# The second block's layer held behind the attention's scores, and its rows' transposes in the layer's own PSUM tiles

## The chip, the cores and the metric

The kernel runs on one NeuronCore of a Trainium2 chip. The metric is the device time of one execution in microseconds (us), lower is better. TensorE is called PE, VectorE DVE, ScalarE ACT, GpSimd POOL and SyncE SP, as in the profile.

## What is computed

Three stages follow each other: an attention over 4 batches of 12 heads (448 tokens, 64 dimensions a head) with a root-mean-square norm on q and k, a gated layer on the 1792 tokens, and a mixture of 8 experts that sends each token to the one with the largest logit.

```python
q_n, k_n = (rmsnorm(q, g_q), rmsnorm(k, g_k))
scores = (1.0 / np.sqrt(64)) * np.matmul(q_n, k_n.transpose(0, 1, 3, 2))
attn = softmax(scores)                       # the row's maximum is subtracted
x = heads_side_by_side(np.matmul(attn, v))   # 1792 x 768
gate = 1.0 / (1.0 + np.exp(-(x @ w_gate)))
x = (gate * (x @ w_val)) @ w_out             # d_ff = 1536
idx = np.argmax(cosine(x, expert_emb) / tau, axis=1)
for e in range(8):
    h = np.maximum(x[idx == e] @ w1[e], 0.0)
    out[idx == e] = gate_w[idx == e, None] * (h @ w2[e])
```

## The kernel before

All products are in float32 precision: a matrix is split into a high and a low part, and three products of parts are summed, so a layer tile is 18 matmuls of 448 columns (six input blocks, three products).

**The attention** (`attention`, L451) works on head pairs g = 0 to 23; six of them are one batch, called a block here. A head pair has eight steps u (four groups of 112 tokens, two heads). The generator yields three times a step. For head pair g the steps are: `maxima` (L364), a first score product whose row maxima DVE takes (tiles m{g}_{u}); at step 7 `shifts` (L372), which transposes the negated maxima on PE (pm{g}) and copies them on ACT into the shift rows X2 (L379, two copies); ten steps later than the maxima, `scores` (L386), two matmuls a step: the score itself (the first half, L392) and the shift with the low part (the second half, L393), after which ACT takes the exponential (L395) into pt{g}_{r}. `weigh` (L413) multiplies four exponentials at a time with v on PE (av{g}, "a weighing" below), and ACT copies the finished one (L429); `over_sums` divides by the sums (rb{g}). For the head pairs that follow, `q_side` and `k_side` transpose the normed q and k (pq, pk), and ACT and DVE copy them into X (L315) and Y (L358, L322); ACT also takes the squares of q and k (L263) and a small sum (ms, L271).

PSUM has eight tiles of one bank each, by tag: "mm" two, "T" three, "S" two, "av" one. The scores alternate between the two tiles of "S": score r takes the tile of score r - 2, which its exponential must have read. The maxima of head pairs 6 and up, pq, pk, pm and rb share the three of "T".

**The layer** of a block (`glu`, L689) runs beside the attention of later blocks: block 0 beside head pairs 6 to 11, block 1 beside 12 to 23. For each of 12 blocks of d_ff it makes two tiles of 18 products (pg{b}_{f}, pv{b}_{f}) in the tag "mm", the gate on ACT and DVE, and then six output tiles (po{b}_{d}) of 36 products each. `rows_of` (L987) turns each output tile, in two halves (px{b}_{d}_{h}), into rows of tokens, with the router's logits beside them; ACT copies the rows (L1004), and SP stores them. The products of all of them are issued by line L684 to L685.

**The third and fourth block** have one layer together (`glu_pair`, L784). Its first seven products for a weight block f are pa11, pa12, pa22, ps2, ps4, ps3 and ps1, nine matmuls each, of weights in four forms a, b, c, d; c and d are sums of weights that DVE forms and ACT casts (wh73c is the second weight block's c). pa11 and pa12 need only the third block's outputs (xhp, xlp); the others need sums of outputs of both blocks (tht, tlt, thb, tlb), the last of them those of head pair 23.

**The order of the work.** A scheduler with a simulated timeline puts the instructions in order for each engine; within an engine they then run in that order. The driver at the end of `tile_kernel` only sets the order in which the work is offered: 288 steps of the attention's generator for block 1, and the layer's 37 steps spread over them:

```python
while done * (ticks + (SLACK1 if b else SLACK)) < (i + 1) * n_side:
    next(side, None)
    done += 1
```

What is offered earlier has precedence, but an instruction whose inputs are not ready is passed by, so the layer's products fill PE wherever the attention waits. `tc.issue_after(x)` makes what is issued inside it, on x's engine, stand behind x in that engine's order; it adds no wait on the chip.

Of the kernel before, what the change touches and what calls it, by code (L numbers as in the profile page):

```python
# [20 lines left out]
B, H, S, D = 4, 12, 448, 64  # L21
CP = 112
NCH = S // CP
NG = 2 * NCH
# [40 lines left out]
SPL = ("AD","AD","AD")  # L65
SLACK = 2
SLACK1 = 50
START = 155
RAT = (4, 5, 13, 17, 26)
R3 = (28, 44)  # L70
# [36 lines left out]
def tile_kernel(ctx, tc, q, k, v, g_q, g_k, w_gate, w_val, w_out, emb, tau, w1, w2, out):  # L107
    nc = tc.nc
# [9 lines left out]
    def psum(tag, bufs, name):  # L118
        return ps.tile([P, 512], F32, tag=tag, name=name, bufs=bufs)
# [10 lines left out]
    last = {}  # L130
# [90 lines left out]
    def stage(g):  # L221
        return 0 if g < H // 2 else 1 if g < H else 2
# [163 lines left out]
    def scores(g, r, st):  # L386

        kc, j = divmod(r, 2)
        s_ = psum("S", 2, f"s{g}_{r}")
        z = slice(kc * CP, (kc + 1) * CP)  # L390
        yh, yl = st["Y"][j]
        nc.tensor.matmul(s_[:CP, :S], lhsT=yh[:, z], rhs=st["X"][j], start=True, stop=False)  # L392
        nc.tensor.matmul(s_[:CP, :S], lhsT=yl[:, z], rhs=st["X2"][j], start=False, stop=True)  # L393
        p_ = a2.tile([CP, S], F32, tag="PT", name=f"pt{g}_{r}", bufs=NPT)
        last["exp"] = nc.scalar.activation(p_, s_[:CP, :S], AF.Exp)  # L395
        st["PT"][j, kc] = p_
        if kc and ADDS[stage(g)][r - 2] == "E":
            st["more"][j].append(p_)
        elif kc:
            eng = {"P": nc.gpsimd, "D": nc.vector}[ADDS[stage(g)][r - 2]]  # L400
            if kc == 1:
                st["sum"][j] = a2.tile([CP, S], F32, tag="sum", name=f"sum{g}_{j}", bufs=NSUM)
            eng.tensor_tensor(st["sum"][j], p_, st["PT"][j, 0] if kc == 1 else st["sum"][j], ALU.add)  # L403
# [47 lines left out]
    def attention():  # L451
# [9 lines left out]
        for t in range(NTICK):  # L461
# [16 lines left out]
            if 0 <= w < np_:  # L478
                scores(w, r, st[w])
# [182 lines left out]
    def step_feed():  # L662
        return next(feeders[-1], 1)

    def feed_to(n):
        while len(fed) < n and step_feed() is None:
            pass
# [21 lines left out]
    def glu(b):  # L689
# [31 lines left out]
        for d in range(NC_):  # L721
            pt = psum("mm", 2, f"po{b}_{d}")
            for h in range(2):
                n = NF // 2
                three(pt, n, S, piece(), gs[h * n:(h + 1) * n], h == 0, h == 1)
                if h == 0:
                    yield
            x2 = gp.tile([P, S], F32, tag="x2", name=f"x2{b}_{d}", bufs=2)
            nc.scalar.activation(x2, pt[:, :S], AF.Copy, scale=0.5)
            xT.append(x2)  # L730
            if d:
                rows_of(b, d - 1, xT[d - 1], ss6, lg)
            yield
        rows_of(b, NC_ - 1, xT[NC_ - 1], ss6, lg)
        side_jobs.append(route_all(b, ss6, lg))
        yield
# [47 lines left out]
    def glu_pair():  # L784
# [66 lines left out]
        for what, *at in pair_order():  # L851
# [23 lines left out]
            if h:  # L875
                ws[d] = w
                if d == 0:

                    steps = [second_steps(t, 0) for t in range(2)]
                    for k in (3 * (NF // 2 - 2), 99):  # L880
                        for m in steps:
                            for _ in zip(range(k), m):
                                pass
                    for t, x2 in enumerate(xT):
                        rows_of(b + t, d, x2, ss6[t], lg[t])
                    xT.clear()
                    yield
                elif d < NC_ - LATE:
                    for t in range(2):
                        rows_of(b + t, d, second_half(t, d), ss6[t], lg[t])  # L890
                        yield
                continue
# [94 lines left out]
    def rows_of(b, d, x2, ss6, lg, later=False):  # L987

        both = state["beside"][d % 2]
        nc.gpsimd.tensor_copy(both[:, P:], state["enT"][:, d])  # L990
        place = ROWS[d] if b == 1 else "r"
        rows = gp.tile([CP, NCH, P], F32, tag="rows", name=f"rows{b}_{d}", bufs=2) if place == "r" else \
            wp.tile([CP, NCH, P], F32, tag={"w": "wr", "s": "sq64"}[place], name=f"rows{b}_{d}", bufs={"w": 3, "s": SQB}[place])
        for h in range(2):
            tp = psum("T", 3, f"px{b}_{d}_{h}")
            z = slice(2 * h, 2 * h + 2)
            t_ = tp[:CP, :2 * (P + E)].rearrange("p (c d) -> p c d", c=2)
            for c in range(2):
                nc.tensor.matmul(t_[:, c], lhsT=x2[:, (2 * h + c) * CP:(2 * h + c + 1) * CP], rhs=both, start=True, stop=True)
            if d == 0:  # L1000
                nc.vector.tensor_copy(lg[:, z], t_[:, :, P:])
            else:
                nc.vector.tensor_tensor(lg[:, z], lg[:, z], t_[:, :, P:], ALU.add)
            nc.scalar.copy(rows[:, z], t_[:, :, :P])  # L1004
        nc.sync.dma_start(x2d[b * S:(b + 1) * S, d * P:(d + 1) * P].rearrange("(p c) d -> p c d", c=NCH), rows)

        def squares():
            rsq = gp.tile([CP, NCH, P], F32, tag="rsq", name=f"rsq{b}_{d}", bufs=1)
            if b:
                nc.scalar.activation(rsq, rows, AF.Square)  # L1010
            else:
                nc.gpsimd.tensor_tensor(rsq, rows, rows, ALU.mult)
            nc.vector.tensor_reduce(ss6[:, :, d:d + 1], rsq, axis=AX.X, op=ALU.add)

        if not later:
            squares()
        return squares
# [494 lines left out]
    def open_pool(name, **kw):  # L1512
        held = ExitStack()
        return held.enter_context(tc.tile_pool(name=name, bufs=2, **kw)), held
# [6 lines left out]
    for i in range(n_first):  # L1521
        next(att)
        if i == SETUP:
            with tc.issue_after(last["exp"].ins):
                router_setup()
        if i >= START and (i - START) % FSP == 0 and len(fed) < LEAD:
            with tc.issue_after(last["max"].ins), tc.issue_after(last["exp"].ins):
                step_feed()
    n_side = 2 * NF + 2 * NC_ + 1
    n_feed = 2 * NF + 2 * NC_  # L1530
    for b in range(2):
        side = glu(b)
        done = given = 0
        per = 6 if b == 0 else 2
        ticks = step * (b + 1)
        for i in range(ticks):
            next(att, None)
            if b == 0 and n_first + i == SETUP:
                with tc.issue_after(last["exp"].ins):
                    router_setup()  # L1540
            if n_first + b * step + i == 3 * (NG * H * B // 2 - 1) + CLOSE:
                a1_held.close()
            while given * ticks < (i + 1) * (n_feed * per + XF * b) and len(fed) < used[0] + LEAD + 1:
                step_feed()
                given += 1
            while done * (ticks + (SLACK1 if b else SLACK)) < (i + 1) * n_side:
                next(side, None)
                done += 1
        more = iter(())
        if b == 1:  # L1550
            for _ in att:
                pass
            a2_held.close()
            s1, s1_held = open_pool("s1", side="right", reuse_waits="tile")
            s2, s2_held = open_pool("s2", reuse_waits="tile")
            more = pair_inputs()
        for _ in side:
            feed_to(used[0] + LEAD)
            next(more, None)
        for _ in more:  # L1560
            pass
# [27 lines left out]
```

## Time and profile before

| what | value |
|---|---|
| time, median of 3 runs | 1205.92 us |
| lowest and highest of them | 1203.11 and 1209.46 us |
| the profiled execution's own time | 1203.91 us |
| its span, first to last instruction | 1202.2 us |
| PE, DVE, ACT, POOL busy | 95%, 70%, 56%, 43% |
| mean granted PE clock | 0.989 |

The span is what the trace shows of the execution; its own time is 1.7 us longer. In the trace a matmul of 448 columns has a duration of about 0.36 us, while the next one starts 0.2 us after it: the starts tell the rate, and idle time is counted only beyond the modelled ends. Stages: block 0's layer ends before 345 us, block 1's layer runs from there to about 625 us, and the pair's layer and the experts follow.

### The profile page before, as it was taken

The numbers are of one execution on the slowest core, as the hardware profiler recorded it, in microseconds if no ns is written. First come the engines' busy times: TensorE is split into PE (matmuls) and PEld (weight loads), VectorE is DVE, ScalarE is ACT, GpSimd is POOL, SyncE is SP. The second block draws the span as 40 slices with busy tenths as digits, with TensorE's granted clock in tenths as the row PEclk, the third lists the DMA queues.
The fourth block names the chain that finished last, engine by engine and source line by source line (L and its number), as shares of the span: only waits on it lengthen the run. The fifth ranks groups of instructions, "written<-read, shape, count | busy, mean of one in ns | idle before, by whom it ended". The sixth has DMA issues, their size and how long they took to land. (4 is left out here: it accounts for less than half of the span.)

```text
span 1202.2 us, 18401 instructions
## 1 busy us (share of the span) xinstructions
PE 1137.4 (95%) x6516; PEld 943.6 (78%) x6517; DVE 844.6 (70%) x1424; ACT 674.2 (56%) x1257; POOL 520.4 (43%) x425
## 2 busy tenths in 40 slices
PE   3998899899889999999998999999999999999996
PEld 2544677677667787776488999999998999999996
DVE  6888888878769866676888984197446566555652
ACT  5889776778665665665764333233323545555552
POOL 4897974679557646545731330043103111111001
PEclk9999899999999999999999999999999999999998
DMA  4212676666733222220131211111255675777763
GB/s 121 62 46 88 209 235 210 195 214 205 228 105 98 87 79 89 89 75 20 43 111 54 80 53 67 40 64 55 73 152 185 180 215 165 231 233 226 213 201 102
DMA packets 151106, 156.15 MB, mean 130 GB/s; under 512 B 6947, under 2 KB 135205, under 8 KB 151010
## 3 DMA queue, kind: packets, MB, share of 16 engines
q1 hardware_dynamic: 148034, 143.07, 39.2%
q0 software_dynamic: 2848, 11.74, 2.8%
q8 instruction: 53, 0.87, 0.3%
q14 instruction: 43, 0.35, 0.1%
q10 hardware_dynamic: 128, 0.11, 0.0%
HBM read 129.74 MB, written 25.91 MB: 129 GB/s over the span
## 5 line engine op out<-in xcount | busy, mean ns | idle before, releaser
L589 DVE TENSOR_TENSOR wl<-wr,wh 128x768 fp32r<-128x768 f32 (+1 forms) x194 | 187.6, 968 | 140.6 <-ACT wh L586 107.0
L586 ACT CAST wh<-wr 128x768 fp32r<-128x768 f32 (+1 forms) x212 | 171.6, 809 | 186.0 <-PE py L685 48.2
L370 DVE TENSOR_REDUCE nm<-m 112x1 fp32r<-112x448 f32 x192 | 114.1, 614 | 32.1 <-PE m L369 30.5
L395 ACT ACTIVATE pt<-s 112x448 f32<-112x448 f32 x192 | 101.2, 541 | 53.8 <-PE s L393 51.2
L403 POOL TENSOR_TENSOR sum<-pt,sum 112x448 f32<-112x448 f32 x78 | 104.1, 1342 | 37.5 <-ACT pt L395 36.9
L272 POOL TENSOR_TENSOR ms<-ms,mhalf 112x8 f32<-112x8 f32 x46 | 84.8, 1843 | 47.1 <-ACT ms L271 46.8
L418 PE MATMUL av<-pt,v 112*64 112x448 f32 x384 | 87.6, 567 | 1.6 <-ACT pt L395 1.6
L369 PE MATMUL m<-Y,X 128*112 128x448 f32 x192 | 72.7, 412 | 14.3 <-ACT X L315 4.9
L403 POOL TENSOR_TENSOR sum<-pt,pt 112x448 f32<-112x448 f32 x48 | 61.0, 1275 | 48.3 <-ACT pt L395 42.8
L392 PE MATMUL s<-X,Y 128*112 128x448 f32 x192 | 78.5, 409 | 2.2 <-ACT pt L395 2.1
L393 PE MATMUL s<-X,Y 128*112 128x448 f32 x192 | 71.7, 381 | 3.3 <-ACT X L379 3.3
L1297 POOL DMA_INDIRECT xe<-x2d,iu_all x16 | 19.0, 1190 | 123.9 <-PE pxe L1322 120.4
L392 PEld LDWEIGHTS s<-X,Y 128*112 128x112 f32 x192 | 34.3, 179 | 40.6 <-issue 31.7
L369 PEld LDWEIGHTS m<-Y,X 128*112 128x112 f32 x192 | 33.7, 182 | 37.9 <-ACT Y L322 8.0
L629 DVE SCALAR_TENSOR_TENSOR wr<-r,wr 128x768 int32<-128x768 int32 x36 | 57.8, 1607 | 0.6
L627 DVE SCALAR_TENSOR_TENSOR wr<-r 128x768 int32<-128x768 int32 x36 | 40.3, 1119 | 24.9 <-ACT r L624 22.3
L1308 POOL DMA_INDIRECT out_dram<-orow,iu_all x16 | 17.9, 1122 | 84.9 <-ACT orow L1429 76.6
L418 PEld LDWEIGHTS av<-pt,v 112*64 112x64 f32 x384 | 22.8, 138 | 36.1 <-issue 23.1
L685 PE MATMUL ph<-xeh,wh 128*128 128x256 f32 (+2 forms) x336 | 50.2, 284 | 0.0
L685 PE MATMUL ph<-xel,wh 128*128 128x256 f32 (+2 forms) x336 | 49.7, 282 | 0.0
L589 POOL TENSOR_TENSOR wl<-wr,wh 128x768 fp32r<-128x768 f32 x18 | 37.5, 2084 | 28.2 <-ACT wh L586 28.1
L685 PE MATMUL ph<-xeh,wl 128*128 128x256 f32 (+2 forms) x336 | 49.4, 282 | 0.0
(776 smaller groups left out, 3039.0 us busy)
## 6 DMA issues: line engine op xcount, KB each, us to landing
wr<-in_w_dram SPq DMA_DIRECT2D x112, 384.0 KB
wr<-w SPq DMA_DIRECT2D x72, 384.0 KB
w<-wr SPq DMA_DIRECT2D x36, 384.0 KB
r<-in_w_gate_dram SPq DMA_DIRECT2D x12, 768.0 KB
r<-in_w_val_dram SPq DMA_DIRECT2D x12, 768.0 KB
r<-in_w_out_dram SPq DMA_DIRECT2D x12, 768.0 KB
wr<-in_w_dram SPq DMA_DIRECT2D x24, 256.0 KB
v<-in_v_dram SPq DMA_DIRECT2D x24, 224.0 KB
```

The source lines that it names most:

```text
L272: nc.gpsimd.tensor_tensor(m, m, mhalf[:CP, :m.shape[1]], ALU.pow)
L369: nc.tensor.matmul(s_[:CP, :S], lhsT=st["X"][j][:, c * CP:(c + 1) * CP], rhs=st["Y"][j][0], start=True, stop=True)
L370: last["max"] = nc.vector.tensor_reduce(st["nm"][:, 2 * c + j:2 * c + j + 1], s_[:CP, :S], axis=AX.X, op=ALU.max, negate=True)
L392: nc.tensor.matmul(s_[:CP, :S], lhsT=yh[:, z], rhs=st["X"][j], start=True, stop=False)
L393: nc.tensor.matmul(s_[:CP, :S], lhsT=yl[:, z], rhs=st["X2"][j], start=False, stop=True)
L395: last["exp"] = nc.scalar.activation(p_, s_[:CP, :S], AF.Exp)
L403: eng.tensor_tensor(st["sum"][j], p_, st["PT"][j, 0] if kc == 1 else st["sum"][j], ALU.add)
L418: beside(*(lambda j=j, kc=kc: nc.tensor.matmul(st["av"][part_of(j), :S], lhsT=st["v"][:, j, kc], rhs=st["PT"][j, kc], start=0 in kcs and k ...
L586: nc.scalar.copy(hi, raw)
L589: eng.tensor_tensor(lo, raw, fv(hi), ALU.subtract)
L629: nc.vector.scalar_tensor_tensor(out=m, in0=high, scalar=-0x80000000, in1=m, op0=ALU.bitwise_and, op1=ALU.bitwise_or)
L685: nc.tensor.matmul(pt[:, :cols], lhsT=wts[i][a], rhs=xs[i][z], start=first and k == 1, stop=last and k == 3 * n)
```

## The change

It has two parts. The halves of `rows_of` for block 1 take their PSUM tile from the tag "mm" (two tiles, the ones in which the layer's products alternate) instead of "T" (three). And the driver keeps a list of marks, one for each step of the attention's generator: the last score matmul (second half) issued by then. In block 1 each step of the layer is issued behind the mark of 24 steps of the generator back, that is of eight scores back; it holds only instructions on the mark's engine, which is PE.

```diff
+AHEAD = 3 * NG
...
-        nc.tensor.matmul(s_[:CP, :S], lhsT=yl[:, z], rhs=st["X2"][j], start=False, stop=True)
+        last["s"] = nc.tensor.matmul(s_[:CP, :S], lhsT=yl[:, z], rhs=st["X2"][j], start=False, stop=True)
...
-            tp = psum("T", 3, f"px{b}_{d}_{h}")
+            tp = psum(*(("mm", 2) if b == 1 else ("T", 3)), f"px{b}_{d}_{h}")
...
+    marks = []
     for b in range(2):
...
             next(att, None)
+            marks.append(last["s"].ins)
...
-                next(side, None)
+                with tc.issue_after(marks[-AHEAD]) if b and len(marks) >= AHEAD else nullcontext():
+                    next(side, None)
                 done += 1
```

The number of instructions is the same; their order differs on every engine, on PE from tile pv1_4 of block 1's layer to the pair's first products. Lines of the change are one to seven higher than those of the kernel before.

PE before, from the transposes of k for head pair 19 to the first maximum of that pair (names: pk transposed k, s{pair}_{step} a score, pm the transposed maxima, pv and po tiles of the layer, av a weighing, m a maximum); rows that only repeat a tile are left out:

```order
L351 MATMUL pk19_4735<-ident_72,kn19_4573 128x112 x4
L392 MATMUL s17_7_4815<-X17_1_4171,Y35_4282 112x448
L393 MATMUL s17_7_4815<-X23_146,Y25_158 112x448
L376 MATMUL pm18_4748<-identr_134,nm0_136 66x112 x4
L685 MATMUL pv1_11_5521<-xh1_4_3510,wh59_5296 128x448
L392 MATMUL s18_0_4827<-X18_0_4403,Y36_4506 112x448
L685 MATMUL pv1_11_5521<-xh1_5_3514,wh59_5296 128x448
L685 MATMUL po1_0_5616<-gh1_0_3631,wh60_5380 128x448
L418 MATMUL av17_4730<-pt17_7_4818,v17_4389 64x448
L393 MATMUL s18_0_4827<-X20_140,Y20_148 112x448
L369 MATMUL m19_0_4761<-Y38_4740,X19_0_4650 112x448
```

Between pm18 and the second half of score 18_0 stood 14 products of pv1_11, nine of po1_0 and the weighing of pair 17. PE in the change, the same place:

```order
L419 MATMUL av17_4730<-pt17_4_4727,v17_4389 64x448
L370 MATMUL m18_7_4721<-Y37_4510,X18_1_4406 112x448
L393 MATMUL s18_1_4842<-X18_1_4406,Y37_4510 112x448
L352 MATMUL pk19_4735<-ident_72,kn19_4573 128x112 x4
L377 MATMUL pm18_4748<-identr_134,nm0_136 66x112 x4
L394 MATMUL s18_0_4827<-X20_140,Y20_148 112x448
L394 MATMUL s18_1_4842<-X21_142,Y21_150 112x448
L370 MATMUL m19_0_4761<-Y38_4740,X19_0_4650 112x448
L393 MATMUL s18_2_4896<-X18_0_4403,Y36_4506 112x448
L394 MATMUL s18_2_4896<-X20_140,Y20_148 112x448
L686 MATMUL pg1_9_5105<-xh1_0_3494,wh54_4890 128x448
```

The layer is at pg1_9 here, where it was at pv1_11 and po1_0; its 17 products follow score 18_2, and nothing of it stands between pm18 and that score. ACT in the change, the same place (xf the copy of a weighing, Y the copies of pk, kn the square of k, X20 and X21 the two copies of pm18, pt the exponential):

```order
L430 COPY xf17_4836<-av17_4730 128x448
L359 CAST Y38_4740<-pk19_4735 64x448
L264 ACTIVATE kn20_4794<-kr20_4585 112x2x4x64
L380 CAST X20_140<-pm18_4748 2x448
L380 CAST X21_142<-pm18_4748 2x448
L323 CAST Y38_4740<-Y38_4740 64x448
L359 CAST Y39_4744<-pk19_4735 64x448
L272 ACTIVATE ms20_4792<-ms20_4792 112x8
L396 ACTIVATE pt18_0_4830<-s18_0_4827 112x448
```

Before, the copies of pk19 and pm18 stood well ahead of the copy of the weighing; now they stand behind it. PE in the change at the start of the pair's layer, where rows that only repeat a tile are left out:

```order
L686 MATMUL po1_5_6204<-gh1_11_5543,wl71_6181 128x448
L1001 MATMUL px1_4_0_6286<-beside0_1247,x21_4_6161 112x136 x2
L686 MATMUL ps20_0_6412<-tht2_0_6129,wh72c_6235 128x448
L686 MATMUL pa220_0_6398<-tht4_0_6139,wh72b_6227 128x448
L686 MATMUL ps30_0_6441<-tht3_0_6134,wh72d_6239 128x448
L686 MATMUL pa221_0_6516<-tht4_0_6139,wh73b_6304 128x448
L686 MATMUL pa110_0_6372<-xhp0_6102,wh72a_6223 128x448
L686 MATMUL pa120_0_6383<-xhp3_6114,wh72a_6223 128x448
L686 MATMUL pa111_0_6490<-xhp0_6102,wh73a_6300 128x448
L686 MATMUL pa121_0_6501<-xhp3_6114,wh73a_6300 128x448
L686 MATMUL ps21_0_6530<-tht2_0_6129,wh73c_6312 128x448
```

Before, pa110 followed po1_5 directly and pa120 and pa111 came next, mixed with the sums' products; now all four tiles of pa11 and pa12 stand between pa221 and ps21.

## Rows read from the trace of the kernel before

**Rows 1.** The page's head: span, and each engine's busy time.
```profile
span 1202.2 us, 18401 instructions
PE 1137.4 (95%) x6516; PEld 943.6 (78%) x6517; DVE 844.6 (70%) x1424; ACT 674.2 (56%) x1257; POOL 520.4 (43%) x425
```

**Rows 2.** Windows: us; busy PE, PEld, DVE, ACT, POOL; PE clock; DMA share; GB/s.
```profile
540.00:550.00 10.00, 10.00 (x53) 8.79 (x53) 5.74 (x10) 4.07 (x9) 2.15 (x2) 1.00 0.08 24
570.00:580.00 10.00, 8.64 (x44) 4.61 (x44) 9.38 (x17) 8.77 (x19) 10.00 (x9) 1.00 0.08 23
640.00:650.00 10.00, 6.87 (x26) 5.87 (x25) 7.52 (x20) 2.85 (x5) 1.40 (x1) 0.83 0.16 40
```

**Rows 3.** Waits of PE, 556 to 602 us: total us, times, longest.
```profile
PE s L393 <- ACT X L379: 2.1, 2, 1.2
PE m L369 <- ACT Y L322: 1.5, 2, 1.2
PE av L418 <- ACT pt L395: 1.0, 2, 0.7
```

**Rows 4.** Timeline of PE, 572 to 576 us: start, us, instruction, idle before.
```profile
572.96 0.39 PE L376 MATMUL pm<-identr,nm 112*66 112x112 f32 x4
...
574.92 0.89 PE L393 MATMUL s<-X,Y 128*112 128x448 f32 x2 [1.20 <-ACT X L379]
```

**Rows 5.** Timeline of ACT, 571 to 575 us.
```profile
571.45 0.52 ACT L358 CAST Y<-pk 64x448 fp32r<-64x448 f32 x1
...
573.79 0.53 ACT L429 COPY xf<-av 128x448 f32<-128x448 f32 x1
574.35 0.95 ACT L379 CAST X<-pm 2x448 fp32r<-2x448 f32 x2
```

**Rows 6.** Timeline of PE, 530 to 540 us.
```profile
530.74 1.38 PE L685 MATMUL po<-gh,wl 128*128 128x448 f32 x6
531.96 0.37 PE L685 MATMUL po<-gh,wh 128*128 128x448 f32 x1
...
533.57 0.38 PE L376 MATMUL pm<-identr,nm 112*66 112x112 f32 x4
533.88 1.72 PE L418 MATMUL av<-pt,v 112*64 112x448 f32 x8
...
536.03 1.39 PE L685 MATMUL po<-gl,wh 128*128 128x448 f32 x6
537.26 1.40 PE L685 MATMUL po<-gh,wl 128*128 128x448 f32 x6
...
539.33 0.56 PE L393 MATMUL s<-X,Y 128*112 128x448 f32 x2
```

**Rows 7.** Timeline of all engines, 596 to 599 us.
```profile
596.34 1.72 PE L418 MATMUL av<-pt,v 112*64 112x448 f32 x8 [0.23 <-ACT pt L395]
...
598.11 0.54 ACT L429 COPY xf<-av 128x448 f32<-128x448 f32 x1 [1.82 <-PE av L418]
```

**Rows 8.** Timelines of PE and of ACT, 580 to 583 us.
```profile
580.78 0.37 PE L393 MATMUL s<-X,Y 128*112 128x448 f32 x1
...
581.25 0.55 ACT L395 ACTIVATE pt<-s 112x448 f32<-112x448 f32 x1 [0.31 <-PE s L393]
```

**Rows 9.** Timeline of PE, 645 to 651 us.
```profile
645.54 1.34 PE L685 MATMUL ps<-tht,wh73c 128*128 128x448 f32 x3 [3.13 <-ACT wh73c L586]
...
648.92 0.88 PE L685 MATMUL ps<-tht,wh72d 128*128 128x448 f32 x3
649.64 0.78 PE L685 MATMUL ps<-tlt,wh72d 128*128 128x448 f32 x3
650.25 0.78 PE L685 MATMUL ps<-tht,wl72d 128*128 128x448 f32 x3
```

**Rows 10.** Timelines of POOL at 650 and of ACT at 655 us.
```profile
650.67 1.02 POOL L1100 TENSOR_TENSOR ss<-ss,half 112x4 f32<-112x4 f32 x1 [7.41 <-DVE ss L1099]
...
655.88 0.23 ACT L1105 ACTIVATE ex<-lg 112x32 f32<-112x32 f32 x1
```

**Rows 11.** Waits of PE, 660 us to the end: the longest.
```profile
PE pxa L1241 <- DMA xea<-x2d,iua: 0.5, 1, 0.5
```

## The prediction

> **What bounds the kernel now.** I read the page first: TensorE (PE) is busy 95% of the 1202.2 us span [rows 1], so the time can move only through PE's idle time and clock. The windows show where the work that this change touches has any [rows 2]: at 540 to 550 us, where the second block's layer runs beside the attention, PE is full; at 570 to 580, where that layer has run far ahead and the attention's last head pairs are alone, it is busy 8.64 of 10 us; at 640 to 650, where the last two blocks' paired layer begins, 6.87 at a granted clock of 0.83. The list of waits names them: 2.1 us for the shift rows X (L379), 1.5 for Y (L322), 1.0 for the exponentials (L395), together 4.6 us between 556 and 602 us [rows 3].
>
> The timeline shows what such a wait is. At the border between two head pairs the shifts `pm` are transposed at 572.96, one maximum follows, and the next score's second half starts only at 574.92, after 1.20 us of idling for ACT [rows 4]. ACT was not waiting for `pm`: it was working through its own row of copies, one started every 0.58 us (571.45 to 574.35, five steps), and the copies of `pm` stand last [rows 5]. The same border earlier costs nothing: `pm` at 533.57, the score's second half at 539.33, and PE was full between, because the layer's products stood there, twelve of them in two of the rows, beside a weighing [rows 6]. A product is 0.203 us on PE (six in 530.74 to 531.96) [rows 6], a whole layer tile of 18 is 3.7 us. The cover is what hides the 2 to 3 us that ACT needs.
>
> **What the order shows.** The hold binds. In the changed order each tile of 18 products stands in one piece (at most one or two split off), directly behind the score that its mark names: pg1_9's mark is the score 18_2, and its first product follows that score's second half. Before, the products lay in the attention's gaps. Now, at the borders of head pairs 15, 17, 18, 19, 20 and 21, the tile that could cover has already run or is not yet allowed, and `pm` and the next scores stand next to each other; borders 16, 22 and 23 keep a weighing or products between. So the gaps of the stretch 556 to 602 are not filled; they are spread over some 190 us ahead of 600.
>
> **The terms.** *Removed:* the waits of the attention's lonely end, 4.6 us [rows 3].
>
> *Added at the borders.* Head pair 18 in full, t = 0 when PE leaves av17. ACT can copy av17 at about 0.1 (in the row, 0.05 us after the weighing's end) [rows 7]. `pk19` ends near 1.05, so Y38 starts at 1.1; behind it, at 0.58 a step [rows 5], the square of k for pair 20 at 1.7, the two copies of `pm18` from 2.3 (0.95 for both) to 3.2, then Y38's second half, Y39, ms20 (0.2) and, at about 4.5, the exponential of score 18_0, which takes 0.55 [rows 8]. Score 18_2 needs the bank that this exponential empties: it starts at 5.0. PE has in that time five matmuls at 0.2 and two groups of four transposes at 0.3 (533.57 to 533.88) [rows 6]: 1.7 us. So 3.3 us of waiting. The same count gives 1.0 at pair 15, 1.9 at 17, 1.6 at 19, 2.1 at 20 and 2.0 at 21: 11.9 us. Ends: six times the dearest single wait shown, 1.20 [rows 4], is 7.2; six times the 3.3 of pair 18 is 20. I keep the count, since it gives the shown 1.20 when applied to that border.
>
> *Added inside head pairs.* Scores 17_4, 22_4 and 23_2 stand behind one score or less since the score whose bank they take. The exponential ends 0.82 us after PE is free of a score (580.98 to 581.80) [rows 8], PE has 0.2 to 0.4 us of work: 0.4, 0.4 and 0.6. And the six casts of the paired layer's inputs stand on ACT between the exponentials 20_2 and 20_3; the weighing of pair 20 then waits about 1.0. Together 2.4; ends 0 and 5.
>
> *The paired layer's start.* There PE waited 3.13 us for the cast of a weight sum and then ran nine products in 3.38 us instead of 1.84 (three in 0.61) at the lower level of its clock [rows 9], 1.2 instead of 2.4 GHz: 4.7 us in all. In the changed order the 36 products (7.4 us) that need none of the summed inputs, pa110 to pa121, no longer come first but stand directly ahead of the one that waited, so they cover that cast; and pair 23's last weighing stands before all of the last layer tile (36 products) instead of before a third of it, so the inputs' chain on DVE begins 24 products, 4.9 us, earlier. A new wait appears: the fourth of these tiles, pa121, needs pa120's bank, which DVE empties only behind the routing's small instructions, with a POOL power of 1.02 us and an ACT exponential of 0.23 between them [rows 10]. I take 1.0 (ends 0 and the 4.7 removed, which would be a full exchange). Net -3.7.
>
> *The rows' transposes.* Each half now takes one of the two banks that the products alternate in, instead of one of three others. The next product tile waits for its copy on ACT. In the order 18 or more products or a weighing lie between such a half and the tile that takes its bank, over 3 us against one copy; nothing, upper end 0.5 per tile, 3 in all. The last two halves keep their banks until ACT has cast four more weights; pa110 starts behind that, level with PE's own arrival, and counts as nothing. The banks given up serve the maxima, whose waits are not in the list [rows 3]: no gain. The stores of the rows are issued earlier on SP and the layer's weight loads later, between the attention's own loads; POOL's subtractions for the layer move behind the attention's sums. None of them is waited for in the list, DMA is 0.08 busy at 540 to 550 and at 570 to 580 [rows 2], and what uses them moved back as far: nothing.
>
> *Sum:* -4.6 + 11.9 + 2.4 - 3.7 = **+6.0 us**. Behind 660 us PE's waits are some tenths each, the longest 0.5 us [rows 11], so whatever is won or lost reaches the end in full. The profiled execution took 1203.91 us, so 1209.9; the median of the three runs is 2.0 above it, 1205.92, and on that footing I say **1212.0 us**.
>
> **Rivals.** *Faster: the even mixture pays.* If ACT reaches each border with an empty queue and the scheduler's placement is right, the borders cost the 0.5 us that a copy of `pm` alone takes (half of 0.95): six times 0.5 is 3.0, the inner waits nothing, and -4.6 + 3.0 - 4.7 gives -6.3: 1199.6. For it: ACT is only 41% busy beside the layer at 540 to 550 [rows 2]. Against: the copies' order on ACT is fixed, and at each of the six borders the copy of the weighing and up to three others stand ahead of those of `pm`. It decides where all added waits stay under 3.3 us. The Trainium skill (Perfetto Trace Analysis, Optimization Strategy) says that a kernel with several regimes may gain by interleaving them, which is what is done here; by that rule the time comes out near this rival. The trace agrees only where the products lie between `pm` and the score [rows 6].
>
> *No measurable change.* The borders overlap more than counted (7.2, the lower end) and the inner waits halve: -4.6 + 7.2 + 1.2 - 3.7 = +0.1, so 1206.
>
> *Slower still: the clock.* After the 3.13 us wait the granted level fell and cost 1.54 us [rows 9]; the 1.20 us wait did not lower it (1.00 at 570 to 580) [rows 2]. Pair 18 idles 3.3 us in four parts with single matmuls between, pairs 17, 20 and 21 about 2. If the level falls at these four, 6.2 us come on top: 1218. It would need these waits to act as that one did. The Trainium skill (TensorE: Matmul & The Clock Gate, A second HAM failure mode) reports a kernel that lost clock to frequent short idling between its matmul groups; by it this rival would be the rule. The trace does not bear it out at 570 to 580, where the wait of 1.20 us lies.
>
> That the hold does nothing is excluded by the order.
>
> **How the numbers follow.** Half a per cent (6.0 us) is about what a measurement of this kernel can tell from no change. My forecast (+3 to +10) has 0.46, of which 0.29 lies beyond +6; no measurable change 0.25; the faster rival 0.15, counted whole as faster though its price lies only just beyond -6; the clock 0.14. So faster 0.15, same 0.17 + 0.25 = 0.42, slower 0.29 + 0.14 = 0.43. The range 1200 to 1220 leaves out the outer half of the two extreme cases, 0.08 and 0.07. The likeliest case alone gives 1209 to 1216.
>
> **What would show it.** Right: the waits of PE between 410 and 610 us sum to about 14 us, the largest for X (L380 then), Y and the exponentials, in groups every 25 us or so, each ahead of a solid tile of layer products; windows there fall from 10.00 to 9.2 or 9.5; the 3.13 us wait for wh73c is gone and the clock at the paired layer's start stays 1.00. Wrong: waits there under 8 us in sum (then faster or equal); a granted clock under 1.00 between 410 and 600 (then the clock rival); or a new wait of 3 us or more in the paired layer's first 30 us, which would take the gain there back.

## The result, and the profile after

The change makes the kernel slower by about 1%: 1216.93 us in the median of 6 runs (1215.76 to 1219.71), against 1206.58 us for six runs of the kernel before; the ratio is 1.0096, 95% interval 1.0079 to 1.0113. The profiled execution took 1215.76 us, its span is 1214.0 us: 11.8 us more than the span before. The head of its page answers to [rows 1]; each engine has as many instructions as before:

```profile
span 1214.0 us, 18398 instructions
...
PE 1140.6 (94%) x6516; PEld 945.4 (78%) x6517; DVE 842.2 (69%) x1424; ACT 676.9 (56%) x1257; POOL 525.6 (43%) x425
```

Two marks frame the changed part in both traces: the routing of the first block (`ppos`, at 405.88 us before and 405.69 now), up to which the order is the same, and the first product with wh78a, the eighth weight block of the paired layer (713.23 and 724.28 us). Between them lie 307.35 us before and 318.59 now, 11.24 more; 0.8 more comes behind, and ahead it is 0.2 less. These are the windows of the kernel after in which PE idles or its clock is under 1.00 most, with the sum of all windows of 10 us from 400 to 730 us, and below it the same sum for the kernel before; the columns are those of [rows 2]:

```profile
490.00:500.00 10.00, 7.75 (x32) 5.94 (x31) 4.16 (x6) 5.95 (x13) 7.05 (x6) 0.83 0.37 108
...
540.00:550.00 10.00, 8.53 (x35) 6.81 (x37) 4.32 (x9) 7.05 (x16) 4.06 (x4) 0.83 0.11 36
...
650.00:660.00 10.00, 7.11 (x29) 6.20 (x28) 6.94 (x25) 3.93 (x8) 1.02 (x1) 0.83 0.22 62
...
sum 330.00, PE 316.58 PEld 249.56 DVE 244.81 ACT 177.73 POOL 159.02; mean PE 9.59 PEld 7.56 DVE 7.42 ACT 5.39 POOL 4.82
...
sum 330.00, PE 322.09 PEld 256.85 DVE 257.43 ACT 179.82 POOL 156.25; mean PE 9.76 PEld 7.78 DVE 7.80 ACT 5.45 POOL 4.73
```

PE idles 330.00 - 316.58 = 13.4 us there, and 330.00 - 322.09 = 7.9 us before. Three windows have a mean clock of 0.83, each 0.17 of 10 us or 1.7 us lost, against one before, at 640 to 650 [rows 2]. So 5.5 us are idle time and 3.4 us clock; 2.3 of the 11.24 stand in neither (where they lie comes out below). The list of PE's waits (from 410 to 612 us, then from 612 to 700; total us, times, longest) says what PE idled for:

```profile
PE s L394 <- ACT X L380: 4.1, 5, 1.3
PE s L393 <- ACT pt L396: 2.6, 5, 0.9
PE pm L377 <- DVE nm L371: 1.5, 3, 0.7
PE m L370 <- ACT Y L323: 1.0, 1, 1.0
PE pq L311 <- DVE nm L371: 0.9, 1, 0.9
...
PE pa L686 <- ACT rows L1006: 2.9, 1, 2.9
```

Up to 612 us the waits sum to 10.4 us (with one of 0.4 for maxima that is left out here), where [rows 3] had 4.6. PE's timeline shows the border of head pair 17, the layer's products ahead of the border of pair 18 and that border itself, and the paired layer's start:

```profile
466.68 0.46 PE L393 MATMUL s<-X,Y 128*112 128x448 f32 x1
...
468.96 0.89 PE L394 MATMUL s<-X,Y 128*112 128x448 f32 x2 [1.20 <-ACT X L380]
469.69 1.39 PE L686 MATMUL pv<-xh,wh 128*128 128x448 f32 x6
...
484.45 1.38 PE L686 MATMUL pv<-xh,wh 128*128 128x448 f32 x6
...
486.88 1.18 PE L686 MATMUL pv<-xh,wl 128*128 128x448 f32 x5
...
491.83 0.41 PE L377 MATMUL pm<-identr,nm 112*66 112x112 f32 x4 [0.73 <-DVE nm L371]
492.85 0.89 PE L394 MATMUL s<-X,Y 128*112 128x448 f32 x2 [0.61 <-ACT X L380]
...
495.09 0.46 PE L393 MATMUL s<-X,Y 128*112 128x448 f32 x1 [0.90 <-ACT pt L396]
...
495.60 2.23 PE L686 MATMUL pg<-xh,wh 128*128 128x448 f32 x6
497.62 2.12 PE L686 MATMUL pg<-xl,wh 128*128 128x448 f32 x6
499.58 1.18 PE L686 MATMUL pg<-xh,wl 128*128 128x448 f32 x5
...
653.12 1.49 PE L686 MATMUL pa<-xhp,wh72a 128*128 128x448 f32 x3 [2.89 <-ACT rows L1006]
```

Pair 17 waits 1.20 us for the copies of `pm`. At pair 18 it is 2.24 us in three parts; then twelve products take 495.60 to 499.58, 3.98 us, where the twelve from 484.45 took 2.43: the lower level of the clock. And the solid tile pg1_9 that would have covered the border runs right behind it. ACT's timeline gives the reason for the waits, and, at 649.73 and 652.70, that for the wait of pa110:

```profile
490.16 0.53 ACT L430 COPY xf<-av 128x448 f32<-128x448 f32 x1 [2.24 <-PE av L419]
491.13 0.53 ACT L359 CAST Y<-pk 64x448 fp32r<-64x448 f32 x1 [0.44 <-PE pk L352]
491.56 0.63 ACT L264 ACTIVATE kn<-kr 112x512 f32<-112x512 f32 x1
492.27 0.94 ACT L380 CAST X<-pm 2x448 fp32r<-2x448 f32 x2
...
494.50 0.98 ACT L396 ACTIVATE pt<-s 112x448 f32<-112x448 f32 x2
...
649.73 0.83 ACT L587 CAST wh73c<-wr 128x768 fp32r<-128x768 f32 x1 [0.58 <-DVE mx L1046]
652.70 0.65 ACT L1006 COPY rows<-px 112x256 f32<-112x256 f32 x2 [2.13 <-DVE wl73c L590]
```

The two copies of `rows` empty the two halves of px1_5, the last output tile's transposes, from the two banks that pa110 and pa120 take next. They wait for DVE's wl73c: the tile that receives the rows comes, by the code (`ROWS`, `rows_of`), from the ring of three buffers in which the weights arrive, and wl73c is the last to read the buffer that it gets.

### The profile page after: what moved, and what is told of

Read it like the earlier page. It is cut to its first block, busy times and chain, and to the rows that moved or that the text cites. A ratio compares the mean times of both kernels' runs of the same rounds, so it can differ in the third digit from the quotient of the medians.

```text
span 1214.0 us, 18398 instructions
## 1 busy us (share of the span) xinstructions
PE 1140.6 (94%) x6516; PEld 945.4 (78%) x6517; DVE 842.2 (69%) x1424; ACT 676.9 (56%) x1257; POOL 525.6 (43%) x425
## 5 line engine op out<-in xcount | busy, mean ns | idle before, releaser
L404 POOL TENSOR_TENSOR sum<-pt,sum 112x448 f32<-112x448 f32 x78 | 110.7, 1425 | 45.9 <-ACT pt L396 44.9
```

## The experiments

Nine kernels ran. **Bare borders** is the theory that the hold takes the products away from where ACT's row of copies needs them, and that the transposes' banks cost only the wait for pa110. Its rivals: **banks** (the transposes tie the products to ACT, and that makes the border waits) and **the lead** (a layer held back to the attention's pace costs time wherever it stands). In the table the stretch is that between the two marks; idle time and clock come from the windows of 10 us from 400 to 730 us as above, so these three columns tell of one profiled execution each. A ratio is to runs of the kernel before that were taken beside it: six with a median of 1206.58 us for the change, 15 of 1205.98 for the runs 1 to 4, 17 of 1204.74 for 5 to 7, and 20 of 1206.03 for 8 and 9.

| kernel | median us | ratio to before, 95% interval | stretch | idle | clock |
|---|---|---|---|---|---|
| before | 1206.58 | | 307.35 | 7.9 | 1.7 |
| the change | 1216.93 | 1.0096, 1.0079 to 1.0113 | 318.59 | 13.4 | 5.1 |
| 1 hold alone | 1215.87 | 1.0084, 1.0054 to 1.0114 | 317.20 | 13.7 | 3.4 |
| 2 transposes alone | 1211.54 | 1.0052, 1.0031 to 1.0072 | 313.66 | 10.1 | 6.8 |
| 3 last tile's in T | 1215.07 | 1.0070, 1.0042 to 1.0098 | 319.02 | 12.8 | 6.8 |
| 4 hold of 48 steps | 1216.15 | 1.0075, 1.0049 to 1.0102 | 316.97 | 13.5 | 5.1 |
| 5 hold at the shifts | 1202.28 | 0.9982, 0.9962 to 1.0002 | 305.77 | 9.2 | 0.0 |
| 6 five half tiles | 1195.49 | 0.9926, 0.9899 to 0.9953 | 297.56 | 1.4 | 0.0 |
| 7 the same, all in T | 1196.11 | 0.9924, 0.9896 to 0.9952 | 297.92 | 1.4 | 0.0 |
| 8 as 5, last tile's in T | 1202.26 | 0.9969, 0.9952 to 0.9986 | 304.98 | 7.5 | 1.7 |
| 9 two borders | 1211.62 | 1.0057, 1.0035 to 1.0079 | 314.60 | 13.1 | 1.7 |

**1. The hold alone.**

```diff
-            tp = psum(*(("mm", 2) if b == 1 else ("T", 3)), f"px{b}_{d}_{h}")
+            tp = psum(*(("mm", 2) if False else ("T", 3)), f"px{b}_{d}_{h}")
```

> The rows' transposes go back to the attention's PSUM tiles; the hold of 24 steps stays. Theory 'bare borders' (the hold strips the head pairs' borders of their products; the transposes' tiles cost only the new wait at the paired layer's start): PE's waits between 410 and 612 us stay at 9 to 12 us and the granted clock falls at one or two borders as in the changed kernel; the paired layer starts with pa110 at once, as before the change, and the wait for wh73c comes back, shorter, 1.5 to 3 us. Time 1213 to 1217. Theory 'banks' (the transposes in the two banks of the products tie the products to ACT, and that makes the border waits): those waits fall under 6 us and the time is 1207 to 1209.

As 'bare borders' has it. The hold alone makes nearly the whole loss, and the banks make none of the border waits. The list of PE's waits from 410 us, and from 612 to 705:

```profile
PE s L394 <- ACT X L380: 4.0, 5, 1.3
...
PE ps L686 <- ACT wh73c L587: 2.9, 1, 2.9
```

The wait for wh73c came back nearly in full, 2.9 us against 3.13 [rows 9].

**2. The transposes alone.**

```diff
-AHEAD = 3 * NG
+AHEAD = 10 ** 6
```

> No hold; the rows' transposes stay in the layer's own PSUM tiles. 'Bare borders': borders 15 to 19 idle nothing; the layer ends at head pair 21 in the order, so the last two pairs are alone and idle 4 to 6 us, as much as before; the wait for the rows' copies at pa110 is gone, since those copies are long done, and the 36 products from pa110 to pa121 stand ahead of the first that needs wh73c, so the 4.7 us of [rows 9] are saved. Time 1200 to 1204, faster than before the change. 'Banks': the border waits stay at 9 us or more, 1213 to 1217.

Half a hit: the borders idle 1.4 us in the list, but the time is 1211.5, above the range, since the paired layer's start became worse instead of better. In the kernel before, the transposes wait for banks of the attention (in its trace block 1's begin at 598.50 us, behind the attention's last maximum at 594.79), and that holds the last two output tiles back into head pair 23. With banks of their own the layer is done at head pair 21, and nothing stands between the attention's last weighing and the casts of the paired layer's inputs. PE's timeline there:

```profile
627.62 0.97 PE L437 MATMUL rb<-sum,one 112*64 112x448 f32 x4 [1.23 <-POOL sum L404]
630.05 0.64 PE L686 MATMUL ps<-tht,wh72c 128*128 128x448 f32 x1 [1.46 <-ACT tht L753]
...
650.10 1.03 PE L686 MATMUL pa<-xhp,wh72a 128*128 128x448 f32 x3 [2.57 <-ACT rows L1006]
```

The window of these 10 us has a mean clock of 0.51, the lower level nearly throughout:

```profile
630.00:640.00 10.00, 7.96 (x20) 6.20 (x21) 9.93 (x19) 6.73 (x15) 0.00 (x0) 0.51 0.01 2
```

The wait for the rows' copies is there too: px1_5 was transposed at head pair 21, but its copies still wait for the weight buffer. I had taken them as long done. The losses of the two parts do not add up: the hold alone costs 9.9 us in the medians, the transposes alone 5.6, both together 10.4.

**3. The last tile's transposes in the attention's banks.**

```diff
-            tp = psum(*(("mm", 2) if b == 1 else ("T", 3)), f"px{b}_{d}_{h}")
+            tp = psum(*(("mm", 2) if b == 1 and d < NC_ - 1 else ("T", 3)), f"px{b}_{d}_{h}")
```

> Everything as in the changed kernel, but the transposes of the last output tile (px1_5) go to the attention's PSUM tiles. If the wait of 2.89 us ahead of pa110 and the nine slow products behind it come from the two banks that px1_5 holds: both are gone, nothing takes their place, and the time falls by 4 to 4.5 us to 1212 to 1213. If something else is as late there (the inputs' casts, wh73c): a wait of 2 us or more stands elsewhere between 638 and 668 us and the time stays within 1 us of the changed kernel's.

The wait for pa110 is gone, and no wait over 0.5 us stands in its place up to 705 us. But at 712 us PE now waits 1.33 us for DVE's zw and the clock falls, and the changed kernel shows neither there. The time fell by 1.9 us in the medians, within the two intervals, not by 4: inconclusive in time. The profile, which is of the slowest of the six runs (1218.55 us), lost more clock than the changed kernel's, at the bare borders of pairs 18 and 20 and at that wait:

```profile
490.00:500.00 10.00, 6.85 (x30) 3.87 (x29) 6.75 (x9) 5.82 (x12) 7.49 (x6) 0.86 0.30 85
540.00:550.00 10.00, 8.53 (x35) 5.93 (x32) 4.87 (x9) 6.37 (x14) 7.29 (x5) 0.83 0.29 86
...
710.00:720.00 10.00, 8.66 (x42) 7.78 (x42) 7.02 (x19) 5.13 (x8) 1.86 (x1) 0.83 0.25 79
```

**4. A hold of 48 steps.**

```diff
-AHEAD = 3 * NG
+AHEAD = 6 * NG
```

> Hold 48 steps back instead of 24 (two head pairs), transposes as in the changed kernel. 'Bare borders': half of the layer's tiles lie as before the change, the later ones in solid pieces; the waits between 410 and 612 us fall from 10.5 to 5 to 8 us; the last output tile is done before head pair 23 ends, so the wait at pa110 is under 1 us. Time 1206 to 1211. 'Banks': waits there unchanged, only the wait at pa110 goes: 1212 to 1213.

The border waits fell as expected (6.7 us up to the attention's end), but the wait at pa110 stayed, 2.6 us, and the time did not fall clearly (seven runs, at 1210.5 to 1211.3 and at 1216.2 to 1217.4; the profile is of one at 1210.7). With the larger lead the last output tile is done before the attention is, and the start of the paired layer is bare as in the second run: waits of 1.47, 1.40 and 0.91 us for the inputs' casts, and this window:

```profile
630.00:640.00 10.00, 6.63 (x19) 5.22 (x20) 9.97 (x27) 7.41 (x16) 0.00 (x0) 0.66 0.12 39
```

So neither lead that was tried is right: the short one bares the borders, the long one the end.

**5. The same pace, held at the shifts.** Each held step stands behind the transposes `pm` of a head pair's shifts, by a table; the tiles' banks are the changed kernel's.

```diff
-AHEAD = 3 * NG
+BEHIND = {11: 15, 12: 16, 13: 16, 14: 16, 15: 17, 16: 17, 17: 18, 18: 18, 19: 18, 20: 19, 21: 19, 22: 19, 23: 20, 24: 20, 25: 21, 26: 21, 27: 22, 28: 22, 29: 22, 30: 23, 31: 23}
...
+            t_ = nc.tensor.transpose(pm[:D + 2, c * CP:(c + 1) * CP].bitcast(F32R), st["nm"][:, 2 * c:2 * c + 2 + D], state["identr"])
+        shifted_at[g] = t_.ins
...
-                with tc.issue_after(marks[-AHEAD]) if b and len(marks) >= AHEAD else nullcontext():
+                with tc.issue_after(shifted_at[BEHIND[done]]) if b and done in BEHIND else nullcontext():
```

> The same pace as in the changed kernel (two to three half tiles a head pair, 21 of them held), but each is held behind the transposes of a head pair's shifts (pm15 to pm23) instead of behind the score of 24 steps back, so that at least 18 products stand between `pm` and the next score's second half at every border; the order at the paired layer's start, with all rows' transposes in the layer's own PSUM tiles, is the changed kernel's. 'Bare borders': PE's idle time from 405 us to the attention's end falls from 10.4 to 1 to 4 us and the granted clock stays at 1.00 there; the wait of 2 to 3 us ahead of pa110 and the slow products behind it stay. Time 1206 to 1210. Rival 'the lead' (a layer held back to the attention's pace costs PE time wherever its products stand, because ACT, DVE and POOL then serve both at once): idle time stays at 8 us or more, 1214 to 1218.

14.6 us less than the change in the medians, a larger gain than the range had, and level with the kernel before. 'The lead' is refuted: the layer runs at the same pace, beside the same engines. Not one wait for X is left. The idle time in the list from 405 to 612 us fell to 5.4 us, less far than the 1 to 4 expected; what is left waits for DVE's maxima, once ahead of `pm` (pair 21) and twice inside head pairs, besides one exponential:

```profile
PE pm L379 <- DVE nm L371: 1.7, 1, 1.7
PE pq L311 <- DVE nm L371: 1.6, 1, 1.6
PE rb L440 <- DVE nm L371: 1.5, 1, 1.5
PE s L396 <- ACT pt L399: 0.7, 1, 0.7
```

At the paired layer's start the wait of 2.89 us is the changed kernel's, but the three products behind it take 0.87 us instead of 1.49; no window from 400 to 730 us is under 1.00. So 1.7 of the 5.1 us of clock that this run has less lie at a wait that its edit left as it was:

```profile
641.60 0.87 PE L689 MATMUL pa<-xhp,wh72a 128*128 128x448 f32 x3 [2.89 <-ACT rows L1009]
```

**6. Five half tiles held at the shifts, the rest free.** The edit is that of the fifth run with a shorter table, and the last tile's transposes are placed as in the third.

```diff
+BEHIND = {26: 19, 27: 20, 28: 21, 29: 22, 30: 23}
```

> The layer runs freely up to its first output tile, as before the change; five half tiles of 18 products (units 26 to 30) are held, one behind the shifts of each of the head pairs 19 to 23; the rows' transposes are in the layer's own PSUM tiles except those of the last output tile. 'Bare borders' with the paired layer's start as the third experiment showed it: the 4.6 us of waits between 556 and 602 us fall to 0 to 2, the waits for wh73c (3.1 us) and for the rows' copies and the slow products behind them are gone: 5 to 9 us less than before the change, 1197 to 1202. If ACT's queue is late at the borders whatever stands there, or if a new wait takes the place at the paired layer's start: 1204 to 1208.

1195.49 us, 0.9926 of before and 21 us under the change: faster than the range had. PE is full from 405 to 690 us; the one wait that the list has from 405 to 705 us is 1.3 us, at 690. Two of the windows:

```profile
570.00:580.00 10.00, 10.00 (x58) 7.62 (x58) 8.96 (x17) 7.82 (x18) 3.94 (x6) 1.00 0.19 60
...
640.00:650.00 10.00, 10.00 (x53) 9.10 (x52) 9.90 (x23) 4.37 (x8) 2.23 (x2) 1.00 0.22 71
```

PE's timeline at the border of head pair 19 shows the cover: 18 products behind `pm`, one maximum among them, and the scores' second halves (L397) start without a wait.

```profile
527.65 0.39 PE L379 MATMUL pm<-identr,nm 112*66 112x112 f32 x4
527.88 1.45 PE L689 MATMUL po<-gh,wh 128*128 128x448 f32 x6
...
531.03 0.37 PE L370 MATMUL m<-Y,X 128*112 128x448 f32 x1
531.24 0.77 PE L689 MATMUL po<-gh,wl 128*128 128x448 f32 x3
531.84 0.57 PE L397 MATMUL s<-X,Y 128*112 128x448 f32 x2
```

**7. The same with all transposes in the attention's banks.** The table of the sixth run with the first run's edit.

> As the run before, but all rows' transposes in the attention's PSUM tiles, as before the change; the order then begins the paired layer with pa110 and reaches the first product with wh73c early, as before. 'Bare borders': border waits as in the run before, 0 to 2 us, but the wait for wh73c, 2 to 3.5 us, and the slow products behind it come back: 1201 to 1205. The difference of the two runs, 3 to 5 us, is what the transposes' tiles are worth at the paired layer's start. If they are worth nothing there, the two runs agree within 1 us.

A miss: 1196.11 us, 0.6 from the sixth run and within both intervals, so that where the transposes lie is worth nothing that shows here. The wait for wh73c did come back, but at 1.2 us, and the clock stayed at 1.00:

```profile
639.10 0.87 PE L689 MATMUL ps<-tht,wh73c 128*128 128x448 f32 x3 [1.25 <-ACT wh73c L590]
```

**8. The fifth run with the last tile's transposes in the attention's banks.** Its one edit is that of the third run.

> The fifth experiment's kernel (holds behind the shifts), with the transposes of the last output tile alone in the attention's PSUM tiles. If the 2.89 us ahead of pa110 is the price of the two banks that px1_5 holds, it goes and nothing takes its place: 2.5 to 3.5 us less than the fifth experiment, about 1199 to 1200. If the paired layer's inputs are as late anyway: a wait of 2 us or more appears elsewhere between 620 and 660 us and the time is within 1 us of the fifth experiment's.

The wait for pa110 goes here too, and no wait of more than 1.3 us stands behind it. The rows' copies themselves still come late, behind the cast of wh73c (ACT's timeline), but no product needs their banks now:

```profile
641.15 0.83 ACT L590 CAST wh73c<-wr 128x768 fp32r<-128x768 f32 x1 [2.79 <-DVE acc L1095]
...
643.84 0.65 ACT L1009 COPY rows<-px 112x256 f32<-112x256 f32 x2
```

The time is the fifth run's in the medians (1202.26 and 1202.28) and 1.6 us under it by the ratios; in the profile the 2.9 us are partly paid back by 0.6 us more at another wait, 0.6 at the wait at 690 us and a fall of the clock at 550 (1.7 us). So what the wait costs is shown in the trace, and what its removal brings is between nothing and 3 us.

**9. Two borders of the changed kernel covered.**

```diff
+BEHIND = {18: 18, 23: 20}
...
-                with tc.issue_after(marks[-AHEAD]) if b and len(marks) >= AHEAD else nullcontext():
+                with tc.issue_after(shifted_at[BEHIND[done]] if done in BEHIND else marks[-AHEAD]) if b and len(marks) >= AHEAD else nullcontext():
```

> The changed kernel with two of its holds moved: pg1_9 is held behind the shifts pm18 instead of the score 18_2, pv1_11 behind pm20 instead of 20_2; each half tile so moves ahead by two or three scores, the rest of the order and the lead stay. 'Bare borders': the waits at the borders of head pairs 18 and 20, 2.2 and 1.7 us in the changed kernel, go, and with them the two falls of the clock in that stretch, 1.7 us each by the windows: 5 to 7 us less than the changed kernel, 1210 to 1212; the waits at the other borders stay. 'The lead': nothing changes beyond 1 us, since the two half tiles run at nearly the same time as before. If the clock falls whatever stands at these two borders, 3 to 4 us less and a granted clock under 1.00 remains between 485 and 550 us.

5.3 us less than the change in the medians, by moving two half tiles, 36 of the layer's 648 products, by two or three scores. That is more than 'the lead' allows. But the profile does not show the saving where 'bare borders' puts it. The waits for X at the two borders are gone, but two waits for maxima of 1.65 and 1.86 us now stand near them, and in the list the two borders idle 1.9 and 2.0 us where they idled 2.2 and 1.5. The waits elsewhere did not stay either: pair 19's fell from 1.31 to 0.34 us, pair 22 has a new one of 0.40. All in all idle time fell by 0.4 us only; the clock gave 3.4. Of the two falls beside the attention the one at pair 18 is gone and the one at pair 20 is not, as the last sentence expected for a clock that falls whatever stands there (its window, then PE's timeline at the two waits):

```profile
540.00:550.00 10.00, 9.53 (x38) 6.21 (x39) 9.83 (x16) 5.62 (x11) 5.94 (x3) 0.83 0.13 41
...
492.13 0.41 PE L380 MATMUL pm<-identr,nm 112*66 112x112 f32 x4 [1.65 <-DVE nm L372]
...
540.32 0.45 PE L371 MATMUL m<-Y,X 128*112 128x448 f32 x1 [1.86 <-DVE nm L372]
```

The other 1.7 us of clock lie at the paired layer's start, where nothing was edited and PE waits the changed kernel's 2.89 us. So this run bears 'bare borders' out in time, and not in its mechanism; that rests on the fifth and sixth.

A version with the last rows' tile in a buffer outside the weights' ring was not run; that this ring is what makes its copies late rests on the code and on the releaser in the trace.

## Where the prediction held, and where it failed

**The side, the place and the mechanism held.** Forecast +6.0 us on the profiled execution, measured +11.8, about twice as much; forecast 1212.0, measured 1216.93, inside the range of 1200 to 1220 and just above the 1209 to 1216 of the likeliest case. All six borders that the order named (15, 17 to 21) idle, and no other by more than 0.5 us in the list; ACT's row at pair 18 is the one that was counted step by step: av, Y, the square of k, the two copies of `pm`. The fifth and sixth runs show that the products' place beside `pm` decides.

**The border term held; the removed waits were taken too small.** The list counts idling only beyond the modelled end of the matmul before, and a matmul that stands alone has a row of 0.46 us (466.68) where in a row of six each takes 0.2. By the starts, pair 17 takes 3.01 us from 466.68 to 469.69 for four matmuls and one group of transposes, 1.1 us of work: 1.9 us lost, as counted, where the list has 1.20. At pair 18 the exponential that was counted to start at 4.5 started at 494.50, 4.46 us after t = 0, and the score behind it at 5.05 instead of 5.0. (The count's work of PE, five matmuls and two groups, is 1.6 us and not 1.7, so its wait is 3.4.) So read, from the weighing to the layer's next product, pairs 15 and 17 to 21 lose 1.5, 1.9, 3.6, 1.8, 2.9 and 2.1 us, 13.8 in sum, where 11.9 was counted; some 0.5 of pair 20's is the lower clock, which its last two matmuls (0.72 and 0.58 us, from 540.53) already show. The list gives them 0.60, 1.20, 2.24, 1.31, 1.46 and 1.32, 8.1 in sum. The waits inside head pairs, 2.4 counted, are 2.3 in the list, and that is luck: the three scores that were named wait 1.0 us instead of 1.4, the weighing of pair 20 does not wait at all, and 1.3 us for DVE's maxima had not been counted. But the 4.6 us that went were taken from the list [rows 3], not by the starts, and so came out too small. In the list the net is +5.8, and if the 2.3 us that stood nowhere are of this kind, it is +8.1 where the sum had +9.7; that would leave some 8 us for what went, a remainder and not a measurement.

**The step that failed is the paired layer's start,** -3.7 in the sum. It rested on this sentence: "The last two halves keep their banks until ACT has cast four more weights; pa110 starts behind that, level with PE's own arrival, and counts as nothing." It cost 2.89 us, and the lower clock behind it 1.7. I had counted ACT's own work ahead of the copies and not what the copies themselves wait for, the weight buffer that DVE reads last, 2.13 us of standing still on ACT. The wait for wh73c did go, as forecast, and this wait took its place: 4.6 us for 4.7, an exchange worth next to nothing where the sum had -3.7. Such an exchange stood in the text as the upper end of another wait, that of pa121, which was counted at 1.0 us and did not come: pa121's products follow without a gap. The third and eighth runs show the cause: with px1_5's banks elsewhere the wait is gone.

**The clock, which the sum put at nothing, cost 3.4 us.** Its rival came true by half: in the profile the level fell at two borders, pairs 18 and 20, not at four. I had given it 0.14 and priced each fall by the one of [rows 9], 1.54; measured 1.7 by the windows. The Trainium skill (TensorE: Matmul & The Clock Gate, A second HAM failure mode) reports lost clock from frequent short idling between groups of matmuls; the trace agrees at pairs 18 and 20 and not at 15, 17, 19 and 21, where single waits of 0.3 to 1.3 us left the clock at 1.00.

**The sum:** +8.1 (waits beside the attention) +3.4 (clock) -0.2 (2.89 for 3.13) makes 11.3 of the stretch's 11.24; it closes because the 2.3 us are what was left over. Against the +6.0 the paired layer's start is 3.5 us worse and the clock 3.4, while the waits beside the attention are 1.6 better, so part of the errors cancelled. The time lies inside the range because the range is 20 us wide; the sum is about half of what was measured. Of the signs named ahead, the level under 1.00 between 410 and 600 us appeared, and the new wait at the paired layer's start came to 2.89 us, just under the 3 that were to show the sum wrong; the waits up to 612 us sum to 10.4 us where 14 was named. That the 2.3 us lie at bare borders, the other kernels bear out: the stretch less idle time and clock is 300.1, 300.1, 299.4 and 299.9 us in the change and the runs 1, 3 and 9, but 296.8, 296.6, 296.1, 296.5 and 295.8 in the runs 2 and 5 to 8, 298.4 in the fourth, which idles less at the borders, and 297.8 before.

**The faster rival** was wrong for this order and right for another. The Trainium skill (Perfetto Trace Analysis, Optimization Strategy) says that interleaving regimes may pay. The sixth run agrees, at 1195.49 us, where the products stand behind `pm`; the fifth, at 1202.28, is level with the kernel before, and the change, which interleaves at the fifth's pace, is at 1216.93.

## What to carry to other kernels

Filler work hides a wait only where it stands in the in-order queue, so a hold belongs on the instruction whose consumer will wait (here the transposes of the shifts), not on one that is a fixed number of steps back; here half a tile at each of five such places was enough, and the kernel was fastest with the rest unheld. Before a PSUM tile moves into another ring, ask what its reader waits for, down to the buffer that the reader writes to, and who takes that bank next. And ask of each wait in the kernel before what it holds back by accident: here the transposes' wait for a bank kept the cover for the attention's end.

## What the runs showed of the hardware

The same wait did not always cost clock. In the changed kernel and in the fifth run PE was full at a clock of 1.00 for the 10 us ahead of the last products before pa110, then idled 2.89 us for the same copies with the same work behind it. In one the next three products took 1.49 us at the lower level, in the other 0.87; in the ninth run, which also waited 2.89 us, 0.90. At the border of pair 18, on the other hand, a fall followed three waits of at most 0.90 us with single matmuls between; in the ninth run one wait of 1.65 us at the same border was followed by none, and one of 1.86 at pair 20 by a fall. Each fall in the changed kernel cost about 1.7 us, one window of 10 us at 0.83; the third run's at pair 18 cost twice that (0.86 and 0.80 in two windows). The mean clock of the change's six runs lies between 0.979 and 0.990, so the falls in one profile are not those of every execution. What decides whether one comes is not settled by these runs; the profile of the sixth run, with a single wait of 1.3 us, has none (1.00 from 400 to 730 us).
